# Reading the moving operands of both feed-forward layers in another order

## The chip, the cores and the metric

The kernel runs on one core of one Trainium2 chip. The metric is the device time of one execution in microseconds, the median over several runs. The profile is of one execution; its times are counted from the first instruction of the program.

## The reference

All arrays are float32; 8 batches, 8 heads, 576 tokens, 64 numbers a head. First comes an attention of two parts, then a mixing layer over tokens, then a feed-forward network over the 512 features.

```python
def _attn_ref(q, k, v):                      # each (8, 8, 576, 64)
    out_d = sm_attn(q_d, k_d, v_d)           # on means over 4 tokens: 144 x 144
    out_up = np.repeat(out_d, 4, axis=2)
    ...                                      # and a window of 7 keys around each token
    return out_up + out_local

def _moe_ref(x, U, V, w_ch1, w_ch2):         # x: (8, 576, 512)
    xt = x.transpose(0, 2, 1)
    h = xt @ U @ V                           # over tokens, rank 32
    u = x + h.transpose(0, 2, 1)
    ch = np.maximum(u @ w_ch1, 0.0) @ w_ch2  # 512 -> 2048 -> 512
    return u + ch
```

## The kernel before

Everything of the network is held with features on the 128 partitions and tokens along them, so no tensor has to be turned between the layers. A batch's 576 tokens are cut into two halves (`t`) of `TN` = 288. For each half, `uH` and `uL` hold the mixed input as a rounded part and the rest, each as 4 chunks (`dc`) of 128 features by 288 tokens; the weights are split likewise (`W1H`, `W1L`, `W2["H"]`, `W2["L"]`). A product is the sum of three matmuls: high by high, high by low, low by high. The type of all these operands is float32r, with 4 bytes a number.

The network goes in steps of one hidden chunk (`fc`, 16 of them, 128 hidden features each). `ffn1` makes 12 matmuls (L884: 4 chunks of features, three products each) into a PSUM tile `ps_h`; in each the weights are the stationary operand and a chunk of `uH` or `uL`, 128 x 288, is the moving one. ScalarE then writes the rectified and rounded `hH` (L891), and VectorE the rest `hL` (L892). `ffn2`, three steps later (`LAG`), makes 12 matmuls (L907): for each of 4 output chunks `e`, three products with `hH` or `hL` moving, added up over all 16 `fc` in the four PSUM tiles `acc0` to `acc3`. After the last `fc` of a half, GpSimd adds `uH` and `uL` into `o1` (L917), VectorE adds the accumulator to it (L920), and a transfer writes it to `out_t` (L923), whose rows are features and whose columns are tokens. There are 8 x 2 x 16 = 256 steps, so 3072 matmuls on each of the two lines.

The attention of later batches runs beside the network. Its scores (L715 and L722, into `ps_b`), its exponentials on ScalarE (L521, `E`), transposes (L535, `ps_t`), products with the values (L548, `ps_a`), its local sums on GpSimd and VectorE (L795 and L800, through `Pt`; ScalarE copies one word of every eight of `Pt`, L789) and its mixing (`ps_hu`, L844; `ps_u`, L859) end in GpSimd's writing of `uL` (L867). Each tile is used with few buffers, and most values go once through memory between two stages.

The order of the instructions on every engine comes from a planner in the kernel: each operation is listed with a duration, a priority and its tiles, and `plan.run()` plays these through and writes them out in the order in which they would start. The planner counts a step of `ffn1` as `PH` = 1.587 us and three matmuls of `ffn2` as `PF` = 0.398 us. Each engine then works through its own list in that order, and waits where an operand is not there.

## Time and profile before

| | |
|---|---|
| median of 3 runs | 1036.33 us (1035.78 to 1036.66) |
| profiled execution, first to last instruction | 1033.0 us |
| TensorE busy with matmuls | 990.1 us, 96% |
| GpSimd / VectorE / ScalarE busy | 54% / 50% / 38% |
| mean granted clock of TensorE | 0.982 |
| memory read and written | 87.78 and 30.75 MB |

The profiled execution has no time of its own beside its span; the median of the runs lies 3.3 us above the span, for what comes before the first and after the last instruction. In the page, a line of a group has the source line, engine, operation, the tiles written and read, the shapes, the count, the busy time and the mean of one, and then the idle time of the engine just before them with what ended it. For a matmul the shape 128\*64 stands for the stationary operand and 116x128 for the moving one. Matmuls overlap, so that the mean of one is longer than the distance between two of them.

### The profile page before, as it was taken

What the parts mean: (1) busy time and instruction counts of PE and PEld (TensorE: products, weight loads), DVE (VectorE), ACT (ScalarE), POOL (GpSimd) and SP (SyncE); (2) the same over time, 40 slices, a digit from 0 to 9 for tenths busy, and PEclk for the clock granted to TensorE, in tenths of its full rate; (3) what the DMA queues carried; (4) which work ended last, traced back from release to release, by engine and by line L of the source; (5) the groups of instructions that cost most, each with busy time, mean ns of one, the idle gap of its engine ahead of it and who ended that gap; (6) DMA issues with size and microseconds to landing.
All of it is one profiled execution on the core that took longest, in us unless ns stands there. A gap on an engine that the chain in (4) does not pass through costs nothing.

```text
span 1033.0 us, 26869 instructions
## 1 busy us (share of the span) xinstructions
PE 990.1 (96%) x10831; PEld 970.6 (94%) x10831; DVE 513.8 (50%) x1018; ACT 389.5 (38%) x1234; POOL 556.2 (54%) x567
## 2 busy tenths in 40 slices
PE   5787889999999999999999999999999999999998
PEld 4677888999999999999999999999999999999998
DVE  6677987655444447545454545445644424211111
ACT  4576454434333334443344332334443232111110
POOL 4854678595655666585665656567675605211010
PEclk9788999999999999999999999999999999999999
DMA  9867764545445456555444453465555231000000
GB/s 291 232 173 204 193 184 104 134 117 125 102 116 121 108 145 151 123 120 144 116 121 115 121 125 87 113 143 155 125 134 131 75 76 35 24 1 23 2 23 24
DMA packets 222612, 120.30 MB, mean 116 GB/s; under 512 B 175492, under 2 KB 198456, under 8 KB 222488
## 3 DMA queue, kind: packets, MB, share of 16 engines
q1 hardware_dynamic: 222488, 118.58, 45.4%
q8 instruction: 85, 1.39, 0.6%
q14 instruction: 39, 0.32, 0.1%
HBM read 87.78 MB, written 30.75 MB: 115 GB/s over the span
## 4 chain that ended last, share of the span: by engine, by line
PE 87%; DVE 6%; ACT 3%; issue 2%; DMA 1%; POOL 1%; SPq 0%; DVEq 0%; ACTq 0%
PE acc L907 38%; PE ps_h L884 37%; PE ps_a L548 3%; PE ps_b L715 2%; PE ps_hu L844 2%; DVE c L343 1%; DVE c L345 1%; PE ps_t L535 1%; PE ps_b L722 1%; DMA w2r<-in_W 1%; PE ps_u L859 1%; PE ps_v L427 1%; PE ps_a L480 1%; DVE c L341 1%; PE ps_ba L651 1%
## 5 line engine op out<-in xcount | busy, mean ns | idle before, releaser
L907 PE MATMUL acc<-hH,W2H 128*128 128x288 f32 x1024 | 309.4, 302 | 0.0
L884 PE MATMUL ps_h<-uH,W1H 128*128 128x288 f32 x1024 | 304.4, 297 | 0.3 <-ACT uH L865 0.3
L884 PE MATMUL ps_h<-uL,W1H 128*128 128x288 f32 x1024 | 303.2, 296 | 0.5 <-POOL uL L867 0.5
L907 PE MATMUL acc<-hH,W2L 128*128 128x288 f32 x1024 | 302.3, 295 | 0.8 <-POOL W2L L350 0.8
L907 PE MATMUL acc<-hL,W2H 128*128 128x288 f32 x1024 | 302.0, 295 | 0.0
L892 DVE SCALAR_TENSOR_TENSOR hL<-ps_h,hH 128x288 fp32r<-128x288 f32 x256 | 116.3, 454 | 373.1 <-ACT hH L891 372.4
L884 PE MATMUL ps_h<-uH,W1L 128*128 128x288 f32 x1024 | 301.8, 295 | 0.0
L795 POOL TENSOR_TENSOR Pt<-vl,at 128x896 f32<-128x896 f32 (+1 forms) x135 | 233.2, 1811 | 97.6 <-DVE acc L800 44.7
L891 ACT ACTIVATE hH<-ps_h 128x288 fp32r<-128x288 f32 x256 | 104.8, 409 | 436.0 <-PE ps_h L884 435.5
L884 PEld LDWEIGHTS ps_h<-uH,W1H 128*128 128x128 f32 x1024 | 193.4, 189 | 0.8 <-ACT uH L865 0.5
L884 PEld LDWEIGHTS ps_h<-uL,W1H 128*128 128x128 f32 x1024 | 193.4, 189 | 0.7 <-POOL uL L867 0.7
L884 PEld LDWEIGHTS ps_h<-uH,W1L 128*128 128x128 f32 x1024 | 193.7, 189 | 0.0
L907 PEld LDWEIGHTS acc<-hH,W2L 128*128 128x128 f32 x1024 | 192.7, 188 | 1.0 <-POOL W2L L350 1.0
L907 PEld LDWEIGHTS acc<-hH,W2H 128*128 128x128 f32 x1024 | 192.6, 188 | 1.1
L907 PEld LDWEIGHTS acc<-hL,W2H 128*128 128x128 f32 x1024 | 193.0, 188 | 0.0
L800 DVE TENSOR_REDUCE acc<-Pt 128x128 f32<-128x1024 f32 (+1 forms) x135 | 145.6, 1104 | 10.9 <-ACT Pt L789 4.6
L836 POOL TENSOR_TENSOR xL<-xL,xH 116x640 fp32r<-116x640 f32 x28 | 43.9, 1566 | 94.8 <-ACT xH L835 85.9
L867 POOL TENSOR_TENSOR uL<-xT,uH 128x288 fp32r<-128x288 f32 x56 | 44.3, 810 | 81.0 <-ACT uH L865 73.9
L917 POOL TENSOR_TENSOR o<-uH,uL 128x288 f32<-128x288 f32 x64 | 49.7, 820 | 53.2 <-DMA out_t<-o 53.2
L506 POOL TENSOR_TENSOR vr<-vr 72x256 f32<-72x256 f32 x54 | 41.0, 760 | 35.6 <-DMA vr<-in_v 32.7
L789 ACT ACTIVATE Pt<-ul 128x128 f32<-128x128 f32 (+1 forms) x135 | 48.7, 444 | 20.2 <-DVE acc L800 13.8
L740 ACT ACTIVATE se<-ps_b 96x114 f32<-96x114 f32 x108 | 38.5, 357 | 46.6 <-PE ps_b L715 29.3
(126 smaller groups left out, 1080.0 us busy)
## 6 DMA issues: line engine op xcount, KB each, us to landing
vl<-in_vp SPq DMA_DIRECT2D x54, 240.0 KB
out_t<-o SPq DMA_DIRECT2D x64, 144.0 KB
w1r<-in_W SPq DMA_DIRECT2D x16, 512.0 KB
w2r<-in_W SPq DMA_DIRECT2D x16, 512.0 KB
Y<-x_s SPq DMA_DIRECT2D x112, 72.0 KB
gT<-in_kT SPq DMA_DIRECT2D x27, 291.0 KB
xL<-x_s SPq DMA_DIRECT2D x28, 280.0 KB
gq<-in_qT SPq DMA_DIRECT2D x27, 288.0 KB
```

The lines of the kernel that those rows point to most:

```text
L506: pool_tt(256, lambda x=x: nc.gpsimd.tensor_tensor(out=x()[:, :, 0:2, :], in0=x()[:, :, 0:2, :], in1=x()[:, :, 2:4, :], op=ALU.add), [x], ...
L740: act(n * KL, lambda p=ps[hh], se=se, n=n, rows=rows: nc.scalar.activation(se()[rows, 0:n].rearrange("p r k -> p (r k)"), p()[rows, 0:n * ...
L789: act(n * D, lambda n=n, ps=ps, Pt=Pt: nc.scalar.activation(Pt()[:, :n, :, 7], ul()[:, ps, :], AF.Copy), [ul], [(Pt, 1)], prio, 0.16)
L795: nc.gpsimd.tensor_tensor(out=Pt()[:, :n, :, 0:7].rearrange("p s d o -> p o s d"), in0=win, in1=at()[:, ps, :].rearrange("p s o -> p o s") ...
L800: dve(8.5 * n * D, lambda n=n, ps=ps, Pt=Pt: nc.vector.tensor_reduce(out=acc()[:, ps, :], in_=Pt()[:, :n], axis=AX.X, op=ALU.add), [(Pt, 0 ...
L836: pool_tt(640, lambda: nc.gpsimd.tensor_tensor(out=xL(), in0=xL().bitcast(F32), in1=xH().bitcast(F32), op=ALU.subtract), [xL, xH], [xL], prio)
L867: pool_tt(TN, lambda uH=uH, uL=uL, uf=uf: nc.gpsimd.tensor_tensor(out=uL()[:, hp, :], in0=uf(), in1=uH()[:, hp, :].bitcast(F32), op=ALU.su ...
L884: nc.tensor.matmul(ps()[:, :TN], w[:, dc, fs], u()[:, dc, :], start=(n == 0), stop=(n == 3 * NDC - 1))
L891: last_h[i] = act(TN, lambda: nc.scalar.activation(hH(), ps()[:, :TN], AF.Relu), [ps], [hH], FIRST, 0.05)
L892: dve(TN, lambda: nc.vector.scalar_tensor_tensor(hL(), ps()[:, :TN], 0.0, hH().bitcast(F32), op0=ALU.max, op1=ALU.subtract), [ps, hH], [hL ...
L907: nc.tensor.matmul(ac[e]()[:, :TN], W2[w][:, fc, es], hx(), start=(fc == 0 and n == 0), stop=(fc == NFC - 1 and n == 2))
L917: pool_tt(TN, lambda e=e, o1=o1: nc.gpsimd.tensor_tensor(out=o1()[:, :TN], in0=uH()[:, e, :].bitcast(F32), in1=uL()[:, e, :].bitcast(F32), ...
```

## The change

`turns` is a view of a row of 288 words as 144 pairs: word 0 and word 144, word 1 and word 145, and so on. Both layers read their moving operand through it. Nothing is moved in memory; each matmul still reads all 288 words of each partition.

The columns of `ps_h`, and with it of `hH` and `hL`, therefore hold the tokens in another order: column 2n + a is token 144a + n. The second layer reads these again through `turns`, so that column 4m + 2b + a of an accumulator is token 144b + 72a + m. The addition on VectorE reads the accumulator in the order of its columns and reads and writes `o1` at the token's place, in steps of 144, 72 and 1 words, so that the output is in the order of tokens. The planner's numbers stay as they are, and each engine gets the same instructions in the same order; in the changed kernel L884 is L888, L907 is L911 and L920 is L925.

```diff
+    def turns(x):
+        return x.rearrange("p (a n) -> p n a", a=2)
+
...
-                    nc.tensor.matmul(ps()[:, :TN], w[:, dc, fs], u()[:, dc, :],
+                    nc.tensor.matmul(ps()[:, :TN], w[:, dc, fs], turns(u()[:, dc, :]),
                                      start=(n == 0), stop=(n == 3 * NDC - 1))
...
-                    nc.tensor.matmul(ac[e]()[:, :TN], W2[w][:, fc, es], hx(),
+                    nc.tensor.matmul(ac[e]()[:, :TN], W2[w][:, fc, es], turns(hx()),
                                      start=(fc == 0 and n == 0), stop=(fc == NFC - 1 and n == 2))
...
-                dve(TN, lambda e=e, o1=o1: nc.vector.tensor_tensor(
-                    out=o1()[:, :TN], in0=ac[e]()[:, :TN], in1=o1()[:, :TN], op=ALU.add),
+                o1v = lambda o1=o1: o1()[:, :TN].rearrange("p (b a m) -> p m b a", b=2, a=2)
+                dve(TN, lambda e=e, o1v=o1v: nc.vector.tensor_tensor(
+                    out=o1v(), in0=ac[e]()[:, :TN].rearrange("p (m b a) -> p m b a", b=2, a=2), in1=o1v(), op=ALU.add),
                     [ac[e], o1], [o1], FIRST)
```

## The prediction

> **What bounds the kernel now.** I read the page first: its lines on busy time, on the granted clock and on the chain that ended last.

> ```profile
> span 1033.0 us, 26869 instructions
> PE 990.1 (96%) x10831; PEld 970.6 (94%) x10831; DVE 513.8 (50%) x1018; ACT 389.5 (38%) x1234; POOL 556.2 (54%) x567
> ...
> PEclk9788999999999999999999999999999999999999
> ...
> PE 87%; DVE 6%; ACT 3%; issue 2%; DMA 1%; POOL 1%; SPq 0%; DVEq 0%; ACTq 0%
> PE acc L907 38%; PE ps_h L884 37%; PE ps_a L548 3%; PE ps_b L715 2%; PE ps_hu L844 2%; DVE c L343 1%; DVE c L345 1%; PE ps_t L535 1%; PE ps_b L722 1%; DMA w2r<-in_W 1%; PE ps_u L859 1%; PE ps_v L427 1%; PE ps_a L480 1%; DVE c L341 1%; PE ps_ba L651 1%
> ```

> TensorE carries the end: 87% of the chain, and 75% of it is the two lines that the change edits, L907 and L884. Next, the groups of instructions, for their count and for the idle time before them.

> ```profile
> L907 PE MATMUL acc<-hH,W2H 128*128 128x288 f32 x1024 | 309.4, 302 | 0.0
> L884 PE MATMUL ps_h<-uH,W1H 128*128 128x288 f32 x1024 | 304.4, 297 | 0.3 <-ACT uH L865 0.3
> L884 PE MATMUL ps_h<-uL,W1H 128*128 128x288 f32 x1024 | 303.2, 296 | 0.5 <-POOL uL L867 0.5
> L907 PE MATMUL acc<-hH,W2L 128*128 128x288 f32 x1024 | 302.3, 295 | 0.8 <-POOL W2L L350 0.8
> L907 PE MATMUL acc<-hL,W2H 128*128 128x288 f32 x1024 | 302.0, 295 | 0.0
> ...
> L884 PE MATMUL ps_h<-uH,W1L 128*128 128x288 f32 x1024 | 301.8, 295 | 0.0
> ```

> There are 6 x 1024 = 6144 such matmuls, with 1.6 us of idle time before all of them. Their mean of 295 to 302 ns is no price, since they overlap; the price is the distance between two starts. For that I asked the order of time in two places, and the granted clock of both (the column after POOL is the clock, then the DMA share).

> ```profile
> 162.11 0.44 PE L907 MATMUL acc<-hL,W2H 128*128 128x288 f32 x1
> ...
> 163.31 0.44 PE L884 MATMUL ps_h<-uH,W1H 128*128 128x288 f32 x1
> ```

> ```profile
> 577.77 0.29 PE L907 MATMUL acc<-hH,W2H 128*128 128x288 f32 x1
> ...
> 583.98 0.29 PE L884 MATMUL ps_h<-uH,W1L 128*128 128x288 f32 x1
> ```

> ```profile
> 162.10:163.40 1.30, 1.30 (x7) 1.30 (x7) 0.59 (x2) 0.44 (x1) 1.30 (x2) 0.50 0.14 7
> 577.70:584.00 6.30, 6.30 (x50) 6.30 (x49) 5.95 (x12) 2.83 (x9) 5.81 (x8) 1.00 0.05 10
> ```

> At half the clock, 5 steps take 1.20 us: 240 ns a matmul, or 0.833 ns for each of 288 columns. At the full clock half of that, 120.0 ns, would be due. But 47 steps take 6.21 us, which is 132.1 ns. Something that doesn't speed up with the array's clock holds it back by 12.1 ns a matmul, and not the traffic of transfers: their share is 0.05 here. A third kind of matmul on the same numbers has 128 columns:

> ```profile
> 304.44 0.46 PE L844 MATMUL ps_hu<-xH,Ust 116*64 116x128 f32 x5
> 304.74 0.46 PE L844 MATMUL ps_hu<-xL,Ust 116*64 116x128 f32 x5
> 305.04 0.35 PE L907 MATMUL acc<-hH,W2H 128*128 128x288 f32 x1
> ```

> Five of these take 0.30 us, 60 ns each. Between 128 and 288 columns lie 72.1 ns, so a column costs 0.451 ns, and 2.3 ns are fixed. Against 0.417 ns a column, the stream is 8% slow: it looks as if columns could not be fetched faster than one in 0.451 ns, and 0.833 ns at the slow clock hides that.

> **The change, part by part.** Each engine has the same instructions in the same order in both kernels; only addresses differ.

> *The moving operand.* The same 288 words a partition are read, but word 0, word 144, word 1, word 145 and so on: no two words that follow each other are neighbours any more. If what limits the stream is the fetch from one place, two places in turn share the load, each having twice the time for its next piece. Then the array's own 0.417 ns a column is left: 120.0 + 2.3 = 122.3 ns, a gain of 9.8 ns a matmul. On the other end, every word could need a fetch of its own. No row shows a matmul reading so; the nearest is ScalarE writing one word in every eight (Pt, L789) beside its copies of neighbouring words:

> ```profile
> L789 ACT ACTIVATE Pt<-ul 128x128 f32<-128x128 f32 x108 | 40.0, 472 | 9.4 <-DMA ul<-up_s 5.8 <-DVE acc L800 3.1
> ...
> L865 ACT ACTIVATE uH<-xT 128x288 fp32r<-128x288 f32 x56 | 21.8, 437 | 11.0 <-DVE xT L862 9.1 <-PE ps_h L884 1.3 <-POOL o L917 0.4
> ...
> L835 ACT ACTIVATE xH<-xL 116x640 fp32r<-116x640 f32 x28 | 20.5, 733 | 3.5 <-DMA xL<-x_s 3.5
> ...
> L789 ACT ACTIVATE Pt<-ul 128x64 f32<-128x64 f32 x27 | 8.9, 329 | 10.8 <-DVE acc L800 10.7
> ```

> Neighbouring words cost (733 - 437) / 352 = 0.84 ns each, scattered ones (472 - 329) / 64 = 2.23 ns: 2.7 times as much. So the bounds are 122.3 ns and 2.7 x 0.451 x 288 + 2.3 = about 350 ns. I take 122.3: the row of ScalarE is a write, by another engine, with one place and not two, while the limit on the stream is the matmuls' own, and half a rate for each place is what the rows at the half clock show to be enough.

> [...]

> *How much of 9.8 ns reaches the end.* By the stretch before 200 us and the rest:

> ```profile
> 0.00:200.00 200.00, 49.53 (x321) 46.25 (x322) 0.91 0.68 189
> 200.00:1033.00 833.00, 402.61 (x2753) 376.55 (x2752) 1.00 0.41 99
> ```

> ```profile
> 0.00:200.00 200.00, 44.15 (x288) 40.11 (x288) 0.91 0.68 189
> 200.00:1033.00 833.00, 419.79 (x2784) 382.67 (x2784) 1.00 0.41 99
> ```

> The first pair is L884, the second L907, and the x behind TensorE's busy time counts its matmuls: 609 before 200 us and about 5535 after. After, each nanosecond saved is one on the path: 5535 x 9.8 = 54.2 us. Before, the clock is 0.91 and TensorE waits for the weights' conversion (the chain's DVE c lines), so I take half: 3.0 us.

> *What it meets when it comes earlier.* The attention's steps stand at fixed places between these matmuls, and their operands must now be ready sooner. One case:

> ```profile
> 502.65 0.43 PE L715 MATMUL ps_b<-gT,gq 64*32 64x38 f32 x12
> ...
> 507.88 0.67 PE L535 MATMUL ps_t<-ident_sb,E 72*72 72x72 f32 x8
> ```

> ```profile
> 507.10 0.21 ACT L521 ACTIVATION_READ_ACCUMULATOR E<-ps_b,nb 72x1 f32 x1
> ```

> The scores end at 503.08, ScalarE's last piece of E at 507.31, the transposes start at 507.88: 0.57 us of margin. The 4.8 us between hold 36 matmuls, which shrink by 0.35 us. So this one holds; others are tighter, and what is late next is E before ps_t. At the half-batches, POOL's last pieces of u come just ahead of their use:

> ```profile
> 338.92 3.87 POOL L867 TENSOR_TENSOR uL<-xT,uH 128x288 fp32r<-128x288 f32 x5
> ```

> ```profile
> 340.31 0.30 PE L884 MATMUL ps_h<-uH,W1H 128*128 128x288 f32 x1
> ```

> The first of these five ends about 0.8 us after 338.92, 0.6 us before the matmuls that may need it. With 768 matmuls a batch, a batch comes 7.5 us sooner; if the attention does not, all of it is lost once. POOL is 54% and DVE 50% busy, so they have room. Between 0 and 7 batches' worth (53 us) I take one, 8 us.

> *The residual addition.* Its 64 DVE instructions read and write o in steps of 72 and 144 words; the accumulators are still read in order.

> ```profile
> L892 DVE SCALAR_TENSOR_TENSOR hL<-ps_h,hH 128x288 fp32r<-128x288 f32 x256 | 116.3, 454 | 373.1 <-ACT hH L891 372.4
> ...
> L920 DVE TENSOR_TENSOR o<-acc,o 128x288 f32<-128x288 f32 x64 | 26.2, 450 | 19.3 <-PE acc L907 19.1
> ```

> Behind it wait the DVE's next work and, through the accumulators, the next half-batch's L907, which comes 12 matmuls of L884 (1.6 us) later. Between 0 and, by ScalarE's scattered words, (2.23 - 0.84) x 288 = 0.4 us each, that margin covers the first; at the worst 64 x 0.4 = 26 us. I take 1 us, mostly for the two that stand behind the last matmul.

> Sum: 54.2 + 3.0 - 8 - 1 = 48 us off the profiled execution's 1033.0 us span, 985 us. The median of the runs shown, 1036.33, lies 3.3 us above that span; I keep that distance: 988 us.

> **Rivals.** *A fetch for every word (slower).* The place is each of the 6144 matmuls; it decides from the point where a column costs over 0.451 ns. If now a fetch brings two words, and then one, a column costs 0.90 ns: 262 ns a matmul, 130 more, 1036 + 798 = 1834 us. By ScalarE's ratio, 350 ns: 1036 + 6144 x 0.218 = 2375 us. For it: L789. Against it: the stream at half the clock has time to spare, and two places could be held open at once.

> *The 8% is not the moving operand's (same).* The matmuls with 128 columns load 64 columns of weights and those with 288 load 128 (the 116\*64 and 128\*128 in the rows). Their excess over 0.417 ns a column, 6.7 and 12.1 ns, fits the weights as well as the columns. If the weights' loading disturbs the stream, order inside the moving operand changes nothing: 1036 us, 1038 with the additions.

> *The gain is real and the attention swallows it.* If the attention's steps cannot come earlier, only the matmuls after its end gain. The last addition of its sums, below, ends near 863 us, so 170 us at 8% remain: 14 us, 1022 us.

> ```profile
> L800 DVE TENSOR_REDUCE acc<-Pt x135: 672/1208/1221, 155.2 to 863.2; 128x128 f32<-128x1024 f32 x108, 128x64 f32<-128x512 f32 x27
> ```

> **How the numbers follow.** Faster 0.55: 0.45 for the forecast, with its own range of 972 (fewer waits and an overhead that falls too) to 1010, and 0.10 for the swallowed gain. The weights' rival has 0.10, and a fetch for every word 0.35, of which 0.21 up to the price of two words a fetch. A measurement of this kernel can tell about 0.2% from no change. The range of 8 in 10 runs from 972 to 1840: it leaves out the dearer part of the slow rival, 0.14, and little below.

> **What would show it.** Right: starts of L888 and L911 about 122 ns apart at a granted clock of 1.00, and still 240 ns at 0.50; the additions near 450 ns. Wrong: starts 260 ns or more apart with TensorE near 100% busy and all other engines' shares down (a fetch for every word); 132 ns as before (weights); 122 ns with idle time before ps_t, ps_hu or ps_h (swallowed).

## The result and the profile after

The changed kernel takes 987.94 us (median of 4 runs, 985.77 to 989.22) against 1036.49 us for the kernel before (median of 4 runs, one more than in the table ahead, 1035.78 to 1039.99): a ratio of 0.9523, 95% interval 0.9501 to 0.9545. It is 48.5 us faster; the prediction was 988 us.

The page after, in the lines that were shown of before: span, busy times, granted clock and the chain that ended last.

```profile
span 987.4 us, 26858 instructions
PE 940.7 (95%) x10831; PEld 918.9 (93%) x10831; DVE 519.7 (53%) x1018; ACT 385.8 (39%) x1234; POOL 539.0 (55%) x567
...
PEclk9779898999999999999999999999999999999999
...
PE 78%; DVE 6%; DMA 5%; ACT 3%; issue 3%; SPq 2%; POOL 2%; DVEq 0%; ACTq 0%
PE acc L911 33%; PE ps_h L888 32%; PE ps_a L548 2%; DMA w2r<-in_W 2%; PE ps_b L715 2%; DVE c L343 2%; PE ps_hu L844 1%; PE ps_v L427 1%; PE ps_t L535 1%; PE ps_b L722 1%; DVE c L345 1%; PE ps_a L480 1%; DVE o L925 1%; PE ps_u L859 1%; DMA s_s<-se 1%
```

TensorE still carries the end. It is busy for 49.4 us less, which is more than the 45.6 us by which the span is shorter. The order of time gives the distance between starts, at the full clock (12 matmuls in a row, first and last) and at half of it (9 steps), with the granted clock of both stretches behind POOL's busy time (0.50 for the one at 104.8 us, 1.00 for the one at 250.6 us).

```profile
250.64 0.29 PE L888 MATMUL ps_h<-uH,W1H 128*128 128x288 f32 x1
...
251.99 0.29 PE L888 MATMUL ps_h<-uH,W1L 128*128 128x288 f32 x1
```

```profile
104.75 0.45 PE L888 MATMUL ps_h<-uL,W1H 128*128 128x288 f32 x1
...
106.91 0.45 PE L888 MATMUL ps_h<-uL,W1H 128*128 128x288 f32 x1
```

```profile
104.80:106.80 2.00, 2.00 (x10) 2.00 (x10) 1.08 (x4) 1.09 (x3) 0.00 (x0) 0.50 0.57 94
250.60:252.10 1.50, 1.50 (x14) 1.50 (x13) 1.50 (x4) 0.00 (x0) 1.50 (x2) 1.00 0.04 4
```

11 steps in 1.35 us are 122.7 ns; the median over all such rows of 12 matmuls of both layers after 250 us is 122.5 ns, where it was 132 in the first layer and 133 in the second. At half the clock it is 0.24 us a step, as before. So the array's own 0.417 ns a column, an estimate as half of the 0.833 that a column costs at half the clock, is now nearly the whole at the full clock too: 288 of them are 120.0 ns, 2.5 under the 122.5 measured, where the kernel before lay 12 to 13 above.

### The profile page after: what moved, and what is told of

Read it like the earlier page. It is cut to its first block, busy times and chain, and to the rows that moved or that the text cites. A ratio compares the mean times of both kernels' runs of the same rounds, so it can differ in the third digit from the quotient of the medians.

```text
span 987.4 us, 26858 instructions
## 1 busy us (share of the span) xinstructions
PE 940.7 (95%) x10831; PEld 918.9 (93%) x10831; DVE 519.7 (53%) x1018; ACT 385.8 (39%) x1234; POOL 539.0 (55%) x567
## 4 chain that ended last, share of the span: by engine, by line
PE 78%; DVE 6%; DMA 5%; ACT 3%; issue 3%; SPq 2%; POOL 2%; DVEq 0%; ACTq 0%
PE acc L911 33%; PE ps_h L888 32%; PE ps_a L548 2%; DMA w2r<-in_W 2%; PE ps_b L715 2%; DVE c L343 2%; PE ps_hu L844 1%; PE ps_v L427 1%; PE ps_t L535 1%; PE ps_b L722 1%; DVE c L345 1%; PE ps_a L480 1%; DVE o L925 1%; PE ps_u L859 1%; DMA s_s<-se 1%
## 5 line engine op out<-in xcount | busy, mean ns | idle before, releaser
L911 PE MATMUL acc<-hH,W2H 128*128 128x288 f32 x1024 | 300.9, 294 | 0.0
L888 PE MATMUL ps_h<-uH,W1H 128*128 128x288 f32 x1024 | 296.5, 290 | 1.1 <-ACT uH L865 1.0
L888 PE MATMUL ps_h<-uL,W1H 128*128 128x288 f32 x1024 | 294.7, 288 | 0.5 <-POOL uL L867 0.5
L888 PE MATMUL ps_h<-uH,W1L 128*128 128x288 f32 x1024 | 294.6, 288 | 0.0
L911 PE MATMUL acc<-hH,W2L 128*128 128x288 f32 x1024 | 293.6, 287 | 0.8 <-POOL W2L L350 0.8
L911 PE MATMUL acc<-hL,W2H 128*128 128x288 f32 x1024 | 293.5, 287 | 0.0
L795 POOL TENSOR_TENSOR Pt<-vl,at 128x896 f32<-128x896 f32 (+1 forms) x135 | 218.6, 1693 | 86.9 <-DVE acc L800 37.2
L888 PEld LDWEIGHTS ps_h<-uH,W1H 128*128 128x128 f32 x1024 | 195.1, 191 | 1.8 <-ACT uH L865 1.3
L888 PEld LDWEIGHTS ps_h<-uL,W1H 128*128 128x128 f32 x1024 | 195.2, 191 | 0.7 <-POOL uL L867 0.7
L911 PEld LDWEIGHTS acc<-hH,W2H 128*128 128x128 f32 x1024 | 194.2, 190 | 1.2 <-ACT W2H L347 0.2
L888 PEld LDWEIGHTS ps_h<-uH,W1L 128*128 128x128 f32 x1024 | 195.1, 191 | 0.0
L911 PEld LDWEIGHTS acc<-hH,W2L 128*128 128x128 f32 x1024 | 194.1, 190 | 1.0 <-POOL W2L L350 1.0
L911 PEld LDWEIGHTS acc<-hL,W2H 128*128 128x128 f32 x1024 | 194.3, 190 | 0.0
L800 DVE TENSOR_REDUCE acc<-Pt 128x128 f32<-128x1024 f32 (+1 forms) x135 | 145.8, 1105 | 18.2 <-ACT Pt L789 9.1
L867 POOL TENSOR_TENSOR uL<-xT,uH 128x288 fp32r<-128x288 f32 x56 | 43.6, 799 | 69.2 <-ACT uH L865 69.1
L789 ACT ACTIVATE Pt<-ul 128x128 f32<-128x128 f32 (+1 forms) x135 | 46.7, 419 | 41.0 <-DVE acc L800 24.0
```

Of the source, the lines that this page charges most:

```text
L789: act(n * D, lambda n=n, ps=ps, Pt=Pt: nc.scalar.activation(Pt()[:, :n, :, 7], ul()[:, ps, :], AF.Copy), [ul], [(Pt, 1)], prio, 0.16)
L795: nc.gpsimd.tensor_tensor(out=Pt()[:, :n, :, 0:7].rearrange("p s d o -> p o s d"), in0=win, in1=at()[:, ps, :].rearrange("p s o -> p o s") ...
L800: dve(8.5 * n * D, lambda n=n, ps=ps, Pt=Pt: nc.vector.tensor_reduce(out=acc()[:, ps, :], in_=Pt()[:, :n], axis=AX.X, op=ALU.add), [(Pt, 0 ...
L867: pool_tt(TN, lambda uH=uH, uL=uL, uf=uf: nc.gpsimd.tensor_tensor(out=uL()[:, hp, :], in0=uf(), in1=uH()[:, hp, :].bitcast(F32), op=ALU.su ...
L888: nc.tensor.matmul(ps()[:, :TN], w[:, dc, fs], turns(u()[:, dc, :]), start=(n == 0), stop=(n == 3 * NDC - 1))
L911: nc.tensor.matmul(ac[e]()[:, :TN], W2[w][:, fc, es], turns(hx()), start=(fc == 0 and n == 0), stop=(fc == NFC - 1 and n == 2))
```

## The experiments

In all of them the moving operands of the two layers are read through `first` and `second`, which stand where `turns` stood (a view of a row `x` of 288 words), and the addition is the plain one of before, so that, but for `pairs_back`, the sums come out in another order of columns and meet the residual of other tokens; `changed_again` alone is the changed kernel as it is. Distances between starts are medians after 250 us of the trace, where the granted clock is 1.00 in the kernel before (to 1020 us) and in the changed one (to 980 us); over their whole profiled executions it is 0.975 to 0.992 on the mean in the runs below. The rows shown are the first and the last of 12 matmuls, 11 steps. Where no ratio is given, the time is of a single execution.

**One layer alone.**

```diff
+    first:  x.rearrange("p (a n) -> p n a", n=144)
+    second: x
```

> Only the first layer reads its moving operand in turns from two places; the second reads in order and the addition is the one of before, so the output's columns stand in another order. If the fetch of neighbouring words holds each matmul back by itself: starts 122.5 ns apart in the first layer and 132.3 in the second, and about half of the 48 us is gained, 1011 to 1014 us. If the weights' loading is what disturbs and the change of the whole stream calms it: both layers somewhere between, 125 to 130 ns.

Measured: 1014.8 us, 0.8 above the range expected, against 1037.0 for the kernel before beside it. First layer, then second:

```profile
254.01 0.28 PE L891 MATMUL ps_h<-uH,W1H 128*128 128x288 f32 x1
...
255.35 0.29 PE L891 MATMUL ps_h<-uH,W1L 128*128 128x288 f32 x1
...
474.38 0.30 PE L914 MATMUL acc<-hH,W2H 128*128 128x288 f32 x1
...
475.84 0.29 PE L914 MATMUL acc<-hH,W2L 128*128 128x288 f32 x1
```

122 and 133 ns: each matmul is held back by its own moving operand, and the rival of the weights, which are loaded alike in both, falls.

**Steps of 2, 4, 8 and 16 words.**

```diff
+    first:  x.rearrange("p (a n) -> p n a", n=4)     # the other kernel: n=8
+    second: x.rearrange("p (a n) -> p n a", n=2)     # the other kernel: n=16
```

> The first layer reads in steps of 4 words (word 0, 4, 8, ... then 1, 5, 9, ...), the second in steps of 2; plain addition, so the output's columns stand in another order. If two far places in turn are what helps: no gain, 132 ns or more in both layers. If any order in which no two neighbours follow each other helps: 122.5 ns in both. [...]

> The first layer reads in steps of 8 words (32 bytes), the second in steps of 16 (64 bytes); plain addition, output's columns in another order. If two far places in turn are what helps: 132 ns or more. If any order without neighbours helps: 122.5 ns in both. [...] If places are told apart by a few address bits (banks): the two steps differ, and the one that stays in one bank is the slower.

Measured: 1795.2 and 1715.5 us. Steps of 4, 2, 8, 16 words, in this order of the rows:

```profile
260.31 0.45 PE L891 MATMUL ps_h<-uH,W1H 128*128 128x288 f32 x1
...
263.18 0.45 PE L891 MATMUL ps_h<-uH,W1L 128*128 128x288 f32 x1
...
295.96 0.45 PE L914 MATMUL acc<-hH,W2H 128*128 128x288 f32 x1
...
298.79 0.44 PE L914 MATMUL acc<-hH,W2L 128*128 128x288 f32 x1
```

```profile
602.74 0.43 PE L891 MATMUL ps_h<-uH,W1H 128*128 128x288 f32 x1
...
605.43 0.43 PE L891 MATMUL ps_h<-uH,W1L 128*128 128x288 f32 x1
...
534.39 0.42 PE L914 MATMUL acc<-hH,W2H 128*128 128x288 f32 x1
...
537.10 0.43 PE L914 MATMUL acc<-hH,W2L 128*128 128x288 f32 x1
```

261, 257, 245 and 246 ns. The dear end of the prediction exists: avoiding neighbours is not enough, and a single place read in steps takes nearly twice the 132 to 133 ns of the plain order. Less 2.5 ns (122.5 less the array's 120.0) that the estimate takes as not depending on the columns, a column costs 0.84 ns in steps of 8 and 16 words and 0.90 in steps of 4. Steps of 8 and 16 cost the same, where by the expectation banks would have made them differ; why steps of 4 cost more, no run tells. The step of 2 words, 257 ns, is hardly cheaper than that of 4.

**Fewer new words.**

```diff
+    first:  x[:, 0:144].unsqueeze(2).broadcast_to([128, 144, 2])
+    second: x[:, 0:1].broadcast_to([128, 288])
```

> The first layer reads each of the first 144 words twice in a row, the second reads one word 288 times: part of the moving operand is left out of the product. If the fetch of new words is the limit: 122.5 ns in both layers, since half as many or no new words are needed; time 980 to 990 us. If the limit is that two reads that follow each other go to the same place: 132 ns or more in both, the second layer worst. If it is neither (an overhead of a long run of columns): 132 ns in both.

Measured: 988.0 us, 123 ns in both layers. The first layer:

```profile
250.50 0.29 PE L891 MATMUL ps_h<-uH,W1H 128*128 128x288 f32 x1
...
251.85 0.29 PE L891 MATMUL ps_h<-uH,W1L 128*128 128x288 f32 x1
```

So a run of 288 columns is not slow by itself, and neither is reading a place twice in a row: the limit lies in bringing words that were not just read.

**Pairs, and two far places without neighbours; two near places; more places.** Two readings of the runs so far were set against each other, theory K and theory B; the first of the expectations below says what each holds.

```diff
+    first:  x.rearrange("p (a n t) -> p n a t", n=2, t=2)         # pairs4_lone
+    second: x.rearrange("p (a n t) -> p t n a", a=2, t=2)
+    first:  x.rearrange("p (c a n) -> p c n a", a=2, n=4)         # pair_4_16
+    second: x.rearrange("p (c a n) -> p c n a", a=2, n=16)
+    first:  x.rearrange("p (a n) -> p n a", n=72)                 # places_4_6
+    second: x.rearrange("p (a n) -> p n a", n=48)
```

> First layer: neighbouring pairs in steps of 4 words (0, 1, 4, 5, 8, 9, ... then the pairs between). Second layer: two places 144 words apart in turn, but in steps of 2 words within each place (0, 144, 2, 146, ... then 1, 145, 3, ...), so that no two neighbours are read near each other. Plain addition; output's columns in another order. Theory K (a fetch brings two neighbouring words and keeps them for a while; one fetch in 0.84 ns, 0.90 if the one before lay within 16 bytes): first layer 131 to 133 ns, second 245. Theory B (one fetch a word, and two far places work in parallel): first layer 245 to 262, second 122.5. [...]

> Two places in turn, as in the change, but near each other: 4 words (16 bytes) apart in the first layer, 16 words (64 bytes) in the second; plain addition; output's columns in another order. Theory K: about 132 ns in the first layer, since fetches follow each other within 16 bytes, and 122 to 124 in the second. Theory B: both places of the first layer lie in one bank if banks are wider than 16 bytes, then 245 to 262; the second 122.5 or 245.

> Four places in turn, 72 words apart, in the first layer, six, 48 words apart, in the second; plain addition; output's columns in another order. Theory K with many fetches kept: 122.5 ns in both; with only two kept: 245 in both, since a pair's second word comes after three or five other fetches. Theory B: 122.5 in both.

Measured: 1396.8, 981.5 and 1202.3 us. Pairs in steps of 4 words, and then the two far places:

```profile
292.54 0.42 PE L891 MATMUL ps_h<-uH,W1H 128*128 128x288 f32 x1
...
295.37 0.44 PE L891 MATMUL ps_h<-uH,W1L 128*128 128x288 f32 x1
...
414.56 0.29 PE L914 MATMUL acc<-hH,W2H 128*128 128x288 f32 x1
...
415.98 0.29 PE L914 MATMUL acc<-hH,W2L 128*128 128x288 f32 x1
```

257 and 129 ns: theory K, which promised 132 and 245, is wrong twice. Theory B had the first right and the second nearly (122.5). But two places only 4 words apart run as fast as two far ones:

```profile
253.25 0.29 PE L891 MATMUL ps_h<-uH,W1H 128*128 128x288 f32 x1
...
254.60 0.29 PE L891 MATMUL ps_h<-uH,W1L 128*128 128x288 f32 x1
```

122.5 ns, and the same at 16 words. Four places in turn take 154 ns and six 167, which neither theory had.

**An order that undoes itself.**

```diff
+    first:  x.rearrange("p (a n t) -> p n a t", n=4, t=2)
+    second: x.rearrange("p (a n t) -> p n a t", n=36, t=2)
```

> The first layer reads neighbouring pairs in steps of 8 words (0, 1, 8, 9, ..., 280, 281, then 2, 3, 10, 11, ...), the second reads pairs from four places 72 words apart in turn, which undoes the order of the first, so that the addition is the plain one of before. Theory K: fetches never follow within 16 bytes and each serves two words, so 122 to 124 ns in both layers; VectorE's addition back at 450 ns; 985 to 989 us, at best 2 us under the changed kernel. Theory B: 245 ns in both, over 1700 us.

Measured: 1792.3 us, ratio 1.725 (1.717 to 1.732); 261 and 255 ns. A miss by theory K, and as a try at a better kernel. The second layer:

```profile
366.61 0.43 PE L914 MATMUL acc<-hH,W2H 128*128 128x288 f32 x1
...
369.42 0.44 PE L914 MATMUL acc<-hH,W2L 128*128 128x288 f32 x1
```

```diff
+    first:  x.rearrange("p (c a n) -> p c n a", a=2, n=2)                # same_line: 0, 2, 1, 3, 4, ...
+    second: x.rearrange("p (a n) -> p n a", n=4)[:, 0:2, :].unsqueeze(3).broadcast_to([128, 2, 72, 2])
+    first:  x.rearrange("p (a n t) -> p n a t", n=2, t=4)                # quads_new
+    second: x.rearrange("p (a m n) -> p n m a", a=2, n=4)                # 0, 144, 4, 148, ...
```

> First layer: two places in turn that are only 2 words apart (0, 2, 1, 3, then 4, 6, 5, 7). Second layer: every fourth word, each twice in a row (0, 0, 4, 4, 8, 8, ...), so half of the moving operand is left out of the product; plain addition. Theory C, made after the last runs (a fetch brings a line of 16 bytes and takes the time of about two columns; the column right behind that wants the same line comes too soon and costs a fetch of its own, the ones after it find the line): 132 ns in the first layer, as for words in order, and 245 to 262 in the second. If the line is 8 bytes: 122.5 in the first. If a column that wants the line of the one before it costs nothing: 122 to 132 ns in the second. If only the number of dimensions or the innermost step of the pattern decides (an innermost pair with a step of 2 or more words is fast, 122.5): 122.5 in the first, and 122.5 in the second, whose innermost step of 0 was fast before.

> First layer: runs of 4 neighbouring words that start 8 words apart (0 to 3, 8 to 11, ...). Second layer: two places 144 words apart in turn, with steps of 4 words within each (0, 144, 4, 148, ...), so that every word is on a line that was not read shortly before; plain addition; output's columns in another order. Theory C (2.0 to 2.2 columns' time for each fetch; the word right behind a fetch on the same line is fetched again): two fetches for 4 words, 124 to 132 ns in the first layer; a fetch for each word, 245 to 262, in the second. If two far places help by themselves: 122.5 in the second. If only a stream without any jump is helped: 245 to 262 in the first.

Measured: 1408.7 and 1407.4 us. The layers of the first, then of the second:

```profile
875.21 0.30 PE L891 MATMUL ps_h<-uH,W1H 128*128 128x288 f32 x1
...
876.66 0.29 PE L891 MATMUL ps_h<-uH,W1L 128*128 128x288 f32 x1
...
1397.28 0.44 PE L914 MATMUL acc<-hH,W2H 128*128 128x288 f32 x1
...
1400.10 0.44 PE L914 MATMUL acc<-hH,W2L 128*128 128x288 f32 x1
```

```profile
554.72 0.31 PE L891 MATMUL ps_h<-uH,W1H 128*128 128x288 f32 x1
...
556.19 0.29 PE L891 MATMUL ps_h<-uH,W1L 128*128 128x288 f32 x1
...
625.13 0.42 PE L914 MATMUL acc<-hH,W2H 128*128 128x288 f32 x1
...
627.96 0.45 PE L914 MATMUL acc<-hH,W2L 128*128 128x288 f32 x1
```

132 and 257 ns, 133 and 257 ns: all four as theory C said, the third 1 ns above its range. Each other reading fails at one of them: two places in turn only 2 words apart gain nothing (132), every fourth word twice in a row is as dear as steps of 2 words (257), and two far places in steps of 4 words are dear too (257). What C does not say is for how long a line is kept. With four places in turn each line of the theory is asked for again after three others, and 154 ns lie between the 122.5 of kept lines and the 245 of lost ones; with six places it is 167. In the second layer of `pairs_back` it is asked for again after three other lines with two words each: kept, it would be two fetches for 4 words, 132 ns, and 255 were measured, a fetch for every word. A line seems not to be kept for long, but no run settles it.

**The scattered addition.** `host_order` reads as the changed kernel does, with the plain addition and the output's columns sorted outside; the residual is then added at other tokens than meant, so it prices the addition and is no version to use.

```diff
-                o1v = lambda o1=o1: o1()[:, :TN].rearrange("p (b a m) -> p m b a", b=2, a=2)
...
+                    out=o1()[:, :TN], in0=ac[e]()[:, :TN], in1=o1()[:, :TN], op=ALU.add),
...
+    outT = outT.reshape(DM, B * S // 288, 72, 2, 2).transpose(0, 1, 3, 4, 2).reshape(DM, B * S)
```

> Both layers read as in the changed kernel, but the addition is the plain one of before and the output is put into the order of tokens when its transposed copy is made outside. If the scattered additions lie beside other work but for the last two: 0.4 to 1 us under the changed kernel, 987 us. If each of the 16 half-batches pays for them through the accumulators that the next one waits for: 4 to 8 us under it, 980 to 984 us.

> The changed kernel once more, beside the one with the plain addition: 0.950 to 0.955 of the kernel before by every theory.

Measured: 986.28 us (ratio 0.9492, 0.9467 to 0.9518) and 986.73 us (0.9507, 0.9482 to 0.9531): no difference that these runs can tell. The groups of VectorE, of `host_order` and of the changed kernel:

```profile
L927 DVE TENSOR_TENSOR o<-acc,o 128x288 f32<-128x288 f32 x64 | 26.0, 449 | 15.9 <-PE acc L914 15.8
```

```profile
L925 DVE TENSOR_TENSOR o<-acc,o 128x288 f32<-128x288 f32 x64 | 39.4, 665 | 14.4 <-PE acc L911 14.3
```

Each addition costs 0.22 us more, 13 us in all, and none of it is seen in the time: in the profiled executions the span ends 4.6 us after the start of the last network matmul in `host_order` and 4.5 us in the changed kernel, so that the additions lie beside TensorE's matmuls. No run gave a version in the right order that beats the changed kernel by more than the runs can tell.

## Why the prediction was right

**The gain of one matmul.** 9.8 ns were forecast, and 122.5 instead of 132 to 133 ns measured. The reason was right in its core, that the fetch of words from one run of neighbours is the limit and the half clock hides it (240 ns in both kernels). It was wrong in "two places in turn share the load": the places needn't be far, 16 bytes are enough (122.5 ns), and two far places alone don't help (257 ns). By theory C what helps is that a line's next word is asked for one column later, and the load is then not shared but halved, from two fetches a line to one: two fetches for 8 words are about 0.22 ns a column, well under the array's 0.417. In this the forecast had luck, since its reason would have promised 122 ns as well for the two far places that take 257. The additions, for which 450 ns were named as a sign of being right, take 665, within the 0 to 0.4 us more that were allowed for each.

**What reaches the end.** Three terms of the sum were off, and cancelled in part. The first matmul of the network starts at 78.2 us before and at 83.4 after (the column behind the durations is first and last start):

```profile
L884 PE MATMUL ps_h<-uH,W1H x1024: 290/294/608, 78.2 to 1023.4; 128*128 128x288 f32 x171
```

```profile
L888 PE MATMUL ps_h<-uH,W1H x1024: 284/286/607, 83.4 to 978.3; 128*128 128x288 f32 x171
```

Nothing ahead of it was changed. By the 610th matmul, at 200.1 and 204.4 us, 4.3 us are still lost, where the sum had 3.0 us gained: 5.3 us are lost ahead of the first of them, and 1.0 gained behind it. From there to the last start the changed kernel wins 49.8 us, 9.0 ns for each of 5534: of 5535 x 9.8 = 54.2 us, 4.4 are lost, where 8 were put in. The additions' 1 us is nothing. So the last start comes 45.5 us earlier (-4.3 + 49.8), and the profiled spans differ by 45.6, where the sum had 48 (3.0 + 46.2 - 1).

That the medians of the runs differ by 48.5 is nearer to the forecast than its terms were, and that 988 was met to the tenth is luck: runs of one kernel differ by more than 3 us. The 3.3 us between the span and the median before are not all what lies outside of the span, either. Runs whose own span is on record lie 1.8 us above it (989.22 and 987.4 us); the other 1.5 us say that the profiled execution of before was a quick one, while that of the changed kernel is the slowest of its four. Of the 4.4 us, 2.7 show as idle time of TensorE; where the other 1.7 went, these rows don't tell. By stretch, before and then after:

```profile
200.00:300.00 100.00, 99.23 (x1060) 98.02 (x1060) 47.07 (x97) 37.46 (x121) 64.61 (x68) 1.00 0.52 128
300.00:800.00 500.00, 500.00 (x5617) 495.38 (x5616) 256.20 (x517) 197.38 (x661) 314.42 (x325) 1.00 0.52 124
```

```profile
200.00:300.00 100.00, 98.03 (x1099) 96.72 (x1099) 52.69 (x103) 41.13 (x138) 67.13 (x72) 1.00 0.56 131
300.00:800.00 500.00, 498.45 (x5853) 492.98 (x5852) 274.94 (x546) 202.51 (x684) 320.78 (x341) 1.00 0.56 130
```

0.8 us of idle time became 3.5. The attention did come earlier, at VectorE's and GpSimd's raised shares: the last addition of its sums starts at 830.3 us, where it was 863.2.

```profile
L800 DVE TENSOR_REDUCE acc<-Pt x135: 671/1209/1223, 162.3 to 830.3; 128x128 f32<-128x1024 f32 x108, 128x64 f32<-128x512 f32 x27
```

So the rival of the swallowed gain did not come true.

**The rivals.** The price of a fetch for every word, an estimate of 262 ns (two words a fetch before, one after), was right: 257 to 261 in steps of 2 and 4 words, 245 and 246 in steps of 8 and 16. ScalarE's ratio, 350 ns, was too dear. The rival did not decide here, by theory C because two places in turn come back to a line. That its line has 4 words, 16 bytes, rests on two runs beside the plain order's 0.45 ns a column: two far places in turn in steps of 2 words take 129 ns (0, 144, 2, 146), as if words two apart shared a fetch, and in steps of 4 words 257 (0, 144, 4, 148), as if words four apart did not. The weights' rival fell with `l1_only`.

## What to carry to other kernels

Compare the distance between matmul starts at two granted clocks: a part that doesn't shrink with the clock is worth a test of how the array is fed; here that is where it lay. For moving operands with 4 bytes a number that are read at the full clock, as here, read two places in turn, 4, 16 or 144 words apart, each in steps of one word: 122.5 ns, where the plain order takes 132 to 133. Pairs and steps take nearly twice the plain order's time (245 to 261 ns), and four or six places 154 and 167 ns. A permutation of columns passes through a chain of layers at no cost until the end, where one scattered addition off the critical path can undo it, as the additions here do (0.22 us more each, and no difference in the time).

## What had not been expected

A step of 2 words and pairs of neighbours take 255 to 261 ns, nearly twice the plain order, although by theory C they use two words of each line in a row. The start of the program varies: the first network matmul comes between 78.2 and 86.2 us in these traces, though nothing ahead of it was changed, with 231 GB/s moved in the first 78 us of the earliest and 215 in those of the latest. The two traces of the changed kernel have it at 83.4 and 83.0; whether chance or the kernel decides it, so few traces do not tell, and so the 5.3 us lost there can't be put down to the change. The single time of `pair_4_16`, 981.5 us, is 4.8 us under `host_order`'s median with the same 122.5 ns, and its network started 3.8 us earlier.
